# A convolution and feed-forward kernel: the order of the first loads of x, w_in, w_out and the softmax weights

## The chip, the cores and the metric

The kernel runs on one NeuronCore of one Trainium2 chip. The metric is the device time of one execution in microseconds (us). Before the change it is 759.16 us, the median of three runs (757.6 to 759.79).

## What is computed

The first stage is a causal convolution whose weights are given for every position and head: seven logits per head go through a softmax, and the seven last rows of `x` are summed with those weights. The second stage is a feed-forward layer with a squared ReLU.

```python
# x: (8, 4096, 192), weight_gen: (8, 4096, 8 heads, 7 taps), float32
w = softmax(weight_gen, axis=-1)
x_pad = concat([zeros(B, 6, D), x], axis=1)          # causal: rows s-6 .. s
out = einsum('bshk,bskhg->bshg', w, x_unf)           # 24 columns per head
# w_in: (192, 2048), w_out: (2048, 192)
h = maximum(out.reshape(32768, 192) @ w_in, 0)
result = (h * h) @ w_out                             # (32768, 192), float32
```

## The kernel before

**Blocks.** The 32768 tokens are cut into 64 sub-blocks of 512. The first two sub-blocks are blocks of their own (block 0 and block 1), and all later blocks hold two (block 2 has sub-blocks 2 and 3). Matmuls run in f16 with sums in float32.

**Softmax.** The logits are worked off in parts (`Softmax`, L146). The first sequence has four parts of 8 rows on each of 128 partitions; s0, s1 and s2 are the first three. A part is loaded (L172, tile `wg`), put through an exponential on ScalarE (L194, `ex`), summed, inverted and scaled on VectorE (L201, L208, L216). The result of a small part lies in `v_first`, that of a large one in `v_big`. Small parts are then copied within SBUF to rows by position (`wr_load_sbuf`, L307, tile `wr`), half of the copies issued by SyncE and half by GpSimd (`move_rows`, L495).

**Conv.** VectorE multiplies `wr` with a band mask (`st_band`, L325), which gives banded matrices `bd`. TensorE multiplies them with `x` in f16 (`st_conv`, L393, into PSUM `yp`), and ScalarE copies the result to `y` (L404). The x tile `xt` comes in one of two ways: sub-blocks 0 and 1 are loaded as float32 by SyncE into `x_st` (`x_load_f32`, L283; L267, L271 and L277) and cast (`x_cast`, L291), the others are loaded and cast at once by a DMA that GpSimd issues (`x_load`, L279).

**Feed-forward.** A unit (`st_unit`, L409) makes 1024 columns of hidden values: matmuls with `w_i` into PSUM `h` (L418; three buffers, which `yp` shares), ReLU on ScalarE (L427, `t`), square on VectorE (L430, `g`). The second matmul (`st_mm2`, L450) sums `g` with `w_o` into PSUM `o`; ScalarE copies and VectorE adds the halves (L464, L465), and the rows are stored. The squares of block j are used by the second matmuls beside the units of block j+1. A string per block sets the order: u is a unit, M half of a second matmul, C the conv of the next block. The first three are `"uuuuuCuuu"`, `"MuMuuuMuuuMCu"` and `"MuuuuMuuuuMuuuuuuuMCu"`.

**What sets the order.** The schedule is written out by hand. Every engine takes its instructions in the order in which the program emits them, and a DMA is issued by an engine's queue when all ahead of it in that queue has been issued and its own waits are met. The lines ahead of the main loop (L516 to L547) emit the start: SyncE loads s0's logits, w_in's first half, x of sub-block 0, w_in's second half. ScalarE casts both halves of w_in (L532), then SyncE copies each half across the partitions (`cross_w_in`, L125), ScalarE casts x of sub-block 0 (L537), and SyncE loads x of sub-block 1 and s1's logits. The buffer of `x_st` is one (tag `ex`), so the second x load waits for the first cast. GpSimd issues row copies, the four parts of w_out (`load_w_out`, L138, a DMA that casts to f16), and clears `v_big`.

**Within the main loop**, a table of due times (`at`, L558) places the pieces of the later softmax parts: s1's exponential ahead of unit 4 of block 0 and its sum and scale ahead of unit 5; s2's logits are loaded ahead of unit 6 of block 0 by SyncE (L592, L619), its exponentials ahead of units 3 and 5 of block 1, its sums and scales ahead of unit 7 of block 1 and unit 0 of block 2. The bands for sub-blocks 2 and 3 come ahead of units 1 and 3 of block 1.

Of the kernel before, what the change touches and what calls it, by code (L numbers as in the profile page):

```python
# [9 lines left out]
def kernel(  # L10
# [25 lines left out]
    nc = tc.nc  # L36
# [52 lines left out]
    w_i = const.tile([P, WQ, 2, NQ + NQ // 2], f16, name="w_i")  # L89
# [22 lines left out]
    x_st = {}  # L112
# [10 lines left out]
    def cross_w_in(q):  # L123
        for r0, r1 in ((0, RT), (RT, 0)):
            nc.sync.dma_start(out=w_i[r0 : r0 + RT, q, 1], in_=w_i[r1 : r1 + RT, q, 0])  # L125
# [11 lines left out]
    def load_w_out(q, n):  # L137
        nc.gpsimd.dma_start(  # L138
            out=w_o[:, q * NF // n : (q + 1) * NF // n],
            in_=moe_w_out[q * Dff // n : (q + 1) * Dff // n].rearrange(  # L140
                "(c p) m -> p c m", p=P
            ),
        )
# [101 lines left out]
    x_t, wr_t, bd_t, yp_t, y_t, g_t, h_t, t1_t, o_t, o_sb_t = ({} for _ in range(10))  # L245
# [17 lines left out]
    def block_load(j, dst, src, width, eng):  # L263
        t0 = (j % NBB) * TB
        first, last = int(t0 == 0), NT
        if first:
            eng.dma_start(out=dst[:, 0], in_=src[0:P, :])  # L267
        a = t0 + tile_start(j, NT - 1)
        if a != t0 + starts[-1]:
            last = NT - 1  # L270
            eng.dma_start(out=dst[:, last], in_=src[a : a + P, :])  # L271
        ap = rows(src, t0 + starts[first], width)
        ap = bass.AP(
            tensor=ap.tensor, offset=ap.offset,
            ap=[ap.ap[0], [STEP * width, last - first], ap.ap[2]],
        )
        eng.dma_start(out=dst[:, first:last], in_=ap)  # L277
# [5 lines left out]
    def x_load_f32(j):  # L283
        x_st[j] = p_one.tile([P, (R + HALO) * HK], f32, name="x_st", tag="ex")
        block_load(
            j, x_st[j][:, 0 : NT * D].rearrange("p (t d) -> p t d", t=NT), x[j // NBB], D, nc.sync
        )

    def x_cast(j, copy):
        x_t[j] = p_x.tile([P, NT, D], f16, name="xt")  # L290
        copy(out=x_t[j].rearrange("p t d -> p (t d)"), in_=x_st[j][:, 0 : NT * D])  # L291
# [6 lines left out]
    def wr_load_sbuf(j, parts, order, engines):  # L298

        wr_t[j] = p_wr.tile([P, NT, HP, SL * 2], f16, name="wr")  # L300
        n = 0
        for i in order:
            t0 = max(j % NBB * TB + tile_start(j, i), 0)
            for s in parts:
                a, b = max(t0, s.t0), min(t0 + P, s.t0 + P * s.r)
                if a < b:
                    engines[n % len(engines)].dma_start(  # L307
                        out=wr_t[j][a - t0 : b - t0, i].rearrange("p g c -> p (g c)"),
                        in_=s.v[
                            (a - s.t0) // s.r : (b - s.t0) // s.r, HALO : HALO + s.r  # L310
                        ].rearrange("p r g c e -> p r (g c e)"),
                    )
                    n += 1
# [170 lines left out]
    with nc.allow_low_precision("fp16 matmul pipeline"), tc.manual_schedule():  # L484
# [25 lines left out]
        def spin(n):  # L510
# [5 lines left out]
        s0, s1, s2 = parts[:3]  # L516
# [3 lines left out]
        w_st = [  # L520
            p_wg.tile([P, (R + HALO) * HK], f32, name="w_st", tag="wg")[:, 0 : NQ + NQ // 2]
            for q in (0, 1)
        ]
# [4 lines left out]
        s0.total(0, s0.rh)  # L528
        s0.recip(0, s0.rh)
        s0.scale(0, s0.rh, nc.vector)  # L530
        for q in (0, 1):
            nc.scalar.copy(out=w_i[:, q, 0], in_=w_st[q])  # L532
        wr_load_sbuf(0, [s0], (0, 2, 1, 4, 3), (nc.sync, nc.gpsimd))
        wr_load_sbuf(1, [s0], range(NT), (nc.gpsimd,))
        for q in (0, 1):
            cross_w_in(q)
        x_cast(0, nc.scalar.copy)  # L537
        x_load_f32(1)
        s1.load(nc.sync)
        for i in (0, 2, 1, 3, 4):  # L540
            st_band(0, (i,))
        st_conv(0)
        st_bands(1)
        x_cast(1, nc.vector.tensor_copy)
        for q in range(4):
            load_w_out(q, 4)
        nc.gpsimd.memset(v_big, 0.0)  # L547


# [8 lines left out]
        def at(j, u, kind, *args):  # L558
            fill.setdefault((j, u), []).append((kind, *args))
# [14 lines left out]
        def exp_time(j, u):  # L574

            if u == 0:
                return j - 1, 5 if j == 2 else 12
            return j, {1: 0, 7: 3, 9: 4, 15: 8}[u]
# [3 lines left out]
        for n, s in enumerate(parts[2:], 2):  # L582
            b, f = s.b, s.fb
            k = n - min(m for m, p in enumerate(parts) if p.b == b)
            times = TIMES.get((b, k)) or (
                (f - 6, 15), (f - 5, 15), (f - 4, 15), (f - 3, 9), (f - 3, 15)
            )
            pieces = [(lo, min(lo + PIECE, s.rh)) for lo in range(0, s.rh, PIECE)]
            for (j, u), (lo, hi) in zip(times, pieces, strict=True):
                at(*exp_time(j, u), "exp", s, lo, hi)  # L590
                at(j, u, "soft", s, lo, hi)
            at(*((0, 6) if n == 2 else (times[0][0] - 1, 0)), "load", s)  # L592
        for j in range(1, NBLK - 1):
            a = BLOCKS[j + 1][0]
            small = [p for p in parts if p.fb <= j + 1][-1].r == FIRST
# [121 lines left out]
```

The softmax here doesn't subtract the row's maximum and nothing guards it: scores larger than these inputs give would overflow.

## Time and profile before

The profile is one execution under the hardware profiler: a span of 759.6 us, all times in us from its start.

| engine | busy, us | share of the span |
|---|---|---|
| PE (TensorE matmul) | 742.6 | 98% |
| DVE (VectorE) | 625.3 | 82% |
| ACT (ScalarE) | 623.5 | 82% |
| POOL (GpSimd) | 87.2 | 11% |

A matmul's end is modelled, so a PE that is busy isn't always at its peak: at half clock it shows as busy as at full clock. Beside the busy time stands the clock that was granted to TensorE, as a share of the full one. SP is SyncE, and a q after an engine's name stands for its queue, which issues DMAs. An arrow `a <- b` in a line of waits reads "a waited for b". The transfers at the start, by the table of DMA issues (median from issue to landing):

| transfer | issued by | count, KB each | us to landing |
|---|---|---|---|
| `w_st` from w_in | SyncE | 2 x 512, 4 x 128 | 5.1, 6.2 |
| `x_st` from x | SyncE | 2 x 384, 2 x 96 | 6.8, 6.0 |
| `w_i` across partitions | SyncE | 4 x 192 | 4.6 |
| `wg` from weight_gen (small parts) | SyncE | 6 x 392 | 4.2 |
| `w_o` from w_out | GpSimd | 4 x 192 | 7.5 |

### The profile page before, as it was taken

What the parts mean: (1) busy time and instruction counts of PE and PEld (TensorE: products, weight loads), DVE (VectorE), ACT (ScalarE), POOL (GpSimd) and SP (SyncE); (2) the same over time, 40 slices, a digit from 0 to 9 for tenths busy, and PEclk for the clock granted to TensorE, in tenths of its full rate; (3) what the DMA queues carried; (4) which work ended last, traced back from release to release, by engine and by line L of the source; (5) the groups of instructions that cost most, each with busy time, mean ns of one, the idle gap of its engine ahead of it and who ended that gap; (6) DMA issues with size and microseconds to landing.
All of it is one profiled execution on the core that took longest, in us unless ns stands there. A gap on an engine that the chain in (4) does not pass through costs nothing.

```text
span 759.6 us, 33610 instructions
## 1 busy us (share of the span) xinstructions
PE 742.6 (98%) x15266; PEld 576.8 (76%) x15266; DVE 625.3 (82%) x1007; ACT 623.5 (82%) x753; POOL 87.2 (11%) x125
## 2 busy tenths in 40 slices
PE   8789999999999999999999999999999999999998
PEld 4666877877787778877877787787778777777787
DVE  5679999899799988888888888898878987777853
ACT  4578898888889888888888888888888888888873
POOL 6222111011100110010100110001100011000000
PEclk9889999999999999999999999999999999999999
DMA  8554525645325544524445433465432454432312
GB/s 213 101 92 79 120 53 103 135 92 113 77 64 113 107 79 59 91 93 83 79 79 121 92 61 51 78 136 99 67 62 40 78 107 79 59 69 53 50 44 65
DMA packets 122394, 65.22 MB, mean 86 GB/s; under 512 B 83881, under 2 KB 118668, under 8 KB 121740
## 3 DMA queue, kind: packets, MB, share of 16 engines
q1 hardware_dynamic: 78012, 46.46, 22.0%
q0 software_dynamic: 44096, 16.53, 20.2%
q8 instruction: 119, 1.95, 1.1%
q14 instruction: 23, 0.19, 0.1%
q10 hardware_dynamic: 144, 0.10, 0.0%
HBM read 48.61 MB, written 28.70 MB: 102 GB/s over the span
## 4 chain that ended last, share of the span: by engine, by line
PE 88%; DVE 4%; DMA 3%; ACT 2%; SPq 1%; issue 1%; DVEq 0%; ACTq 0%
PE o L450 42%; PE h L418 40%; PE yp L393 6%; DMA wg<-in_weight_gen_dram 2%; DVE g L430 2%; ACT t L427 1%; DVE bd L325 1%; DMA w_st<-in_moe_w_in_dram 1%; DMA vd<-v_big 1%; SPq L307 0%; DVE o_sb L465 0%; DVE rcp L208 0%; DVE ssum L201 0%; SPq L118 0%; DVE v_big L216 0%
## 5 line engine op out<-in xcount | busy, mean ns | idle before, releaser
L427 ACT ACTIVATE t<-h 128x1024 f16<-128x1024 f32 x512 | 497.4, 1027 | 68.7 <-PE h L418 68.6
L430 DVE TENSOR_TENSOR g<-t 128x1024 f16<-128x1024 f16 x512 | 335.1, 688 | 102.6 <-ACT t L427 99.7
L450 PEld LDWEIGHTS <-g 64*128 64x128 f16 x8192 | 357.0, 94 | 51.9 <-issue 4.0
L450 PE MATMUL o<-w_o,g 64*128 64x192 f16 x8192 | 387.4, 243 | 1.8 <-issue 1.0
L418 PE MATMUL h<-y,w_i 64*128 64x512 f16 (+1 forms) x3168 | 381.9, 372 | 5.4 <-ACT t L427 3.8
L418 PEld LDWEIGHTS <-w_i 64*128 64x128 f16 x3168 | 176.5, 95 | 108.6 <-issue 7.1
L325 DVE TENSOR_TENSOR bd<-wr,mask 128x4160 f16<-128x4160 f16 (+3 forms) x89 | 149.5, 1703 | 4.8 <-DMA wr<-v_first 4.8
L277 POOL DMA_DIRECT2D xt<-in_x_dram x62 | 51.3, 832 | 450.4 <-PE yp L393 427.5
L464 ACT COPY o_sb<-o 128x384 f32<-128x384 f32 x129 | 62.3, 483 | 32.9 <-PE o L450 32.9
L465 DVE TENSOR_TENSOR o_sb<-o,o_sb 128x384 f32<-128x384 f32 x129 | 71.2, 552 | 10.1 <-ACT o_sb L464 7.8
L404 ACT CAST y<-yp 128x1024 f16<-128x1024 f32 (+1 forms) x64 | 48.2, 805 | 15.3 <-PE yp L393 15.3
L393 PE MATMUL yp<-bd,xt 128*32 128x104 f16 (+8 forms) x3864 | 52.3, 211 | 5.0 <-DVE xt L291 4.1
L393 PEld LDWEIGHTS <-xt 128*32 128x32 f16 (+3 forms) x3864 | 47.0, 93 | 10.8 <-issue 5.0
L194 ACT ACTIVATE ex<-wg 128x448 f32<-128x448 f32 (+2 forms) x44 | 27.3, 619 | 10.3 <-DMA wg<-in_weight_gen_dram 10.3
L216 DVE TENSOR_TENSOR v_big<-ex,rcp 128x112 f16<-128x112 f32 (+1 forms) x136 | 27.4, 264 | 2.1 <-DMA vd<-v_big 0.9
L201 DVE TENSOR_REDUCE ssum<-ex 128x64 f32<-128x448 f32 (+2 forms) x44 | 26.1, 594 | 2.5 <-ACT ex L194 2.5
L208 DVE RECIPROCAL rcp<-ssum 128x64 f32<-128x64 f32 (+2 forms) x44 | 23.7, 539 | 1.5
L307 POOL DMA_DIRECT2D wr<-v_first x31 | 16.8, 563 | 27.1 <-DVE v_first L216 27.1
L267 POOL DMA_DIRECT2D xt<-in_x_dram x7 | 3.8, 548 | 137.5 <-PE yp L393 137.5
L512 PE MATMUL wp<-warm 128*128 128x512 f16 x42 | 11.6, 446 | 1.3 <-DVE warm L504 1.3
L512 PEld LDWEIGHTS <-warm 128*128 128x128 f16 x42 | 4.6, 112 | 7.7 <-issue 3.0
L216 DVE TENSOR_TENSOR v_first<-ex,rcp 128x112 f16<-128x112 f32 (+1 forms) x48 | 9.1, 256 | 0.3
(16 smaller groups left out, 23.9 us busy)
## 6 DMA issues: line engine op xcount, KB each, us to landing
out_dram<-o_sb SPq DMA_DIRECT2D x63, 384.0 KB, 3.0
xt<-in_x_dram POOLq DMA_DIRECT2D x42, 240.0 KB, 6.3
wg<-in_weight_gen_dram SPq DMA_DIRECT2D x4, 1064.0 KB, 8.2
xt<-in_x_dram POOLq DMA_DIRECT2D x20, 192.0 KB, 5.4
wr<-vd SPq DMA_DIRECT2D x38, 80.0 KB, 4.0
vd<-v_big SPq DMA_DIRECT2D x5, 512.0 KB, 5.7
wg<-in_weight_gen_dram SPq DMA_DIRECT2D x6, 392.0 KB, 4.2
wg<-in_weight_gen_dram SPq DMA_DIRECT2D x3, 616.0 KB, 4.0
```

Of the source, the lines that this page charges most:

```text
L194: nc.scalar.activation(out=self.ex[:, lo:hi].rearrange("p r g k e -> p (r g) k e"), in_=self.wg[:, lo:hi].rearrange("p r (g e) k -> p (r g ...
L216: eng.tensor_tensor(out=bass.AP(tensor=v.tensor, offset=v.offset + lo * H * SL + lo % SL * 2 + g * SL * 2, ap=[list(v.ap[0]), [H * SL + 2, ...
L277: eng.dma_start(out=dst[:, first:last], in_=ap)
L325: nc.vector.tensor_tensor(out=bd_t[j][:, H * lo : H * (lo + len(tiles) * n)].rearrange("p (g m c) -> p g m c", g=shape[1], c=2 * SL), in0= ...
L393: nc.tensor.matmul(out=yps[k // per][p0 : p0 + m, col + a : col + b], lhsT=x_t[s][:, i, 32 * q : 32 * q + m], rhs=bd[:, h // 2, h % 2, a - ...
L404: nc.scalar.copy(out=y[:, k0:k1, 0:th], in_=yp[:, 0 : (k1 - k0) * th].rearrange("p (k c) -> p k c", c=th),)
L418: nc.tensor.matmul(out=h[:, half, jj * th : (jj + 1) * th], lhsT=w_in_chunk(u * per + jj, slot, half), rhs=y_t[j][r0 : r0 + RT, k, 0:th], ...
L427: nc.scalar.activation(out=t1, in_=h, func=ActF.Relu)
L430: nc.vector.tensor_tensor(out=g, in0=t1, in1=t1, op=AluOp.mult)
L450: nc.tensor.matmul(out=oo[:, cc * Dm : (cc + 1) * Dm], lhsT=g[r0 : r0 + RT, cc * P : (cc + 1) * P], rhs=w_o[r0 : r0 + RT, fc, :], start=(f ...
L464: nc.scalar.copy(out=o_sb, in_=o[0][:, c])
L465: nc.vector.tensor_tensor(out=o_sb, in0=o[1][:, c], in1=o_sb, op=AluOp.add)
```

## The change

The first loads are put in another order. ScalarE casts only w_in's first half ahead of x; the cast of x of sub-block 0 comes next, SyncE loads x of sub-block 1 behind the first half's crossing, and only then are w_in's second half cast and crossed. w_out is loaded in two pairs of parts. A memset of one column of the x tile of sub-block 0 ahead of the first pair makes GpSimd wait until the conv of block 0 has read that tile; a memset of one column of the second `x_st` ahead of the second pair makes it wait until that x has landed and been cast. Nothing reads the cleared columns afterwards. s2's logits are loaded by GpSimd behind w_out and no longer by SyncE in the main loop; the parts after it are loaded as before. The aim is to have x of sub-block 1 and the logits of s1 and s2 there before they are due, with w_out out of their way.

```diff
@@ -528,22 +528,28 @@
         s0.total(0, s0.rh)
         s0.recip(0, s0.rh)
         s0.scale(0, s0.rh, nc.vector)
-        for q in (0, 1):
-            nc.scalar.copy(out=w_i[:, q, 0], in_=w_st[q])
+        nc.scalar.copy(out=w_i[:, 0, 0], in_=w_st[0])
         wr_load_sbuf(0, [s0], (0, 2, 1, 4, 3), (nc.sync, nc.gpsimd))
         wr_load_sbuf(1, [s0], range(NT), (nc.gpsimd,))
-        for q in (0, 1):
-            cross_w_in(q)
+        cross_w_in(0)
         x_cast(0, nc.scalar.copy)
         x_load_f32(1)
+        nc.scalar.copy(out=w_i[:, 1, 0], in_=w_st[1])
+        cross_w_in(1)
         s1.load(nc.sync)
         for i in (0, 2, 1, 3, 4):
             st_band(0, (i,))
         st_conv(0)
         st_bands(1)
         x_cast(1, nc.vector.tensor_copy)
-        for q in range(4):
+
+        nc.gpsimd.memset(x_t[0][:, 0, 0:1], 0.0)
+        for q in (0, 1):
             load_w_out(q, 4)
+        nc.gpsimd.memset(x_st[1][:, 0:1], 0.0)
+        for q in (2, 3):
+            load_w_out(q, 4)
+        s2.load(nc.gpsimd)
         nc.gpsimd.memset(v_big, 0.0)
@@ -589,7 +595,8 @@
-            at(*((0, 6) if n == 2 else (times[0][0] - 1, 0)), "load", s)
+            if n > 2:
+                at(times[0][0] - 1, 0, "load", s)
```

## The prediction

> **What bounds the kernel now.** I read the page first (engine rows, slices), then the busy time by stretches, then the waits of the first 70 us, the chain of the first 80 us, and the timeline of SyncE and GpSimd. The page's first part and the table by stretches (columns: length; busy PE, PEld, DVE, ACT, POOL; PE clock; DMA share; GB/s):
>
> ```profile
> PE 742.6 (98%) x15266; PEld 576.8 (76%) x15266; DVE 625.3 (82%) x1007; ACT 623.5 (82%) x753; POOL 87.2 (11%) x125
> ```
>
> ```profile
> 15.00:20.00 5.00, 3.89 (x60) 3.10 (x59) 1.85 (x2) 4.08 (x5) 2.96 (x2) 1.00 1.33 235
> 20.00:25.00 5.00, 1.15 (x64) 1.15 (x68) 1.86 (x4) 0.85 (x2) 0.00 (x0) 0.81 0.75 169
> 25.00:30.00 5.00, 5.00 (x74) 3.80 (x66) 4.86 (x14) 4.56 (x6) 0.00 (x0) 0.51 0.02 3
> 35.00:40.00 5.00, 2.53 (x54) 2.20 (x49) 4.70 (x4) 0.85 (x2) 0.47 (x1) 1.00 1.25 244
> 40.00:45.00 5.00, 3.70 (x44) 3.41 (x43) 3.76 (x6) 4.39 (x6) 0.00 (x0) 0.51 0.08 20
> 100.00:740.00 640.00, 638.79 (x13312) 496.71 (x13310) 539.45 (x849) 543.92 (x658) 55.43 (x74) 1.00 0.42 82
> ```
>
> From 100 us on TensorE idles 1.2 us in 640: no edit of the loads can bring anything there. What is to be had lies before 70 us: two holes in TensorE's work (20 to 24, 37.5 to 41), each followed by some 6 us at half clock. The waits of the first 70 us (total, times, longest) name both:
>
> ```profile
> ACT ex L194 <- DMA wg<-in_weight_gen_dram: 10.3, 3, 4.2
> DVE xt L291 <- DMA x_st<-in_x_dram: 6.3, 1, 6.3
> PE yp L393 <- DVE xt L291: 4.1, 1, 4.1
> PE h L418 <- ACT t L427: 3.8, 1, 3.8
> ```
>
> The chain (start, length, what) and SyncE's timeline say when those transfers were issued:
>
> ```profile
> 12.81 0.46 SPq L125
> 13.31 0.60 SPq L125
> 14.01 0.53 SPq L271
> 14.58 0.49 SPq L277
> 15.12 9.15 DMA wg<-in_weight_gen_dram
> 24.38 0.95 ACT ex L194
> ```
>
> ```profile
> 34.52 0.59 SPq L172 DMA_DIRECT2D wg<-in_weight_gen_dram  x1
> ```
>
> Hole 1: the second x is issued at 14.01 and 14.58, behind the crossing of w_in's second half, which waits for its cast (12.78). It lands 8.5 us later (23.1); the cast on VectorE (L291) and the conv of block 1 wait. s1's weights, issued at 15.12, land at 24.3, and ScalarE, in order, stands at their exponential. Hole 2: s2's weights are issued at 34.52, behind SyncE's copies of s1's rows, which wait until s1 is scaled (30.22); they land at 39.7, and ScalarE stands 4.15 us at that exponential while TensorE waits for its PSUM.
>
> **What the skill says.** "TensorE: Matmul & The Clock Gate", What's actually happening: half clock after an idle window of about 3.4 us, full clock after as much busy time. The trace agrees in kind: idle of 4.07 and 3.77 us is followed by 0.50 from 23 to 29.5 and from 40.4 to 46.9; the idle 0.9 us at 12.8 is not. "DMA: Bandwidth & Descriptors", Issuing engines are not separate DMA queues: all issuers share the same 16 DMA engines. The trace agrees: from 15 to 20 us the GpSimd queue took 89.8% and SyncE's 41.5%, together the 1.33 above. The same page's SWDGE vs HWDGE vs iDMA: only GpSimd can cast in a DMA, and its rings and SyncE's are served in turn. w_out, cast to f16, is what fills GpSimd's queue there.
>
> **The change, part by part.**
>
> *x cast ahead of w_in's second cast.* x_st(0)'s large part is issued at 3.60 and lands after 5.1: 8.7. ScalarE finishes the first w_in cast at 7.27+1.47 = 8.74, casts x until 9.73, and stands ready before w_in's second half lands (11.24). So the reordering costs ScalarE nothing. The conv of block 0 ends as before, at about 14.6: its last band ends at 14.15.
>
> *x of the second sub-block earlier.* It shares x_st's buffer, free at 9.73 instead of 13.68. SyncE is at its three row copies until 10.31, then the first crossing until 11.55; x is issued at 11.6 and 12.15, 2.4 us earlier. Landing: 5.1 us as for the first x (beside full traffic) to 6.5, since two crossings (768 KB) are in flight too, but no w_out: 17.3, bounds 17 and 20. The second crossing then starts at 12.8 as before (its cast ends 12.78), and units 4 to 7 alone need it.
>
> *s1's weights.* Issued at 13.95 instead of 15.12. Landing: with no other large transfer 4.2 us (the median), before 9.15; two of four w_out parts join at 14.9. I take 6 us: 20.0; bounds 18 and 22.
>
> *w_out in two parts.* Two memsets of one column, 0.10 us each (the row of the 128x1 constants). The first waits for the conv of block 0 (14.65): parts 0 and 1 are issued 14.8 to 16.5 (0.80 each). The second waits for VectorE's cast of x(1): bands of block 1 end at 16.84, x lands 17.3, cast 0.66, so 18.0; parts 2 and 3 issued until 19.8. Queued behind it on GpSimd: s2's load, the memset of v_big (2.53), then s1's row copies (not due before 26.1) and x of block 2. Landing 4.5 to 9.5 us as before: part 1 by 23.5, part 3 by 27. The users are the first second-matmuls of block 0 (23.7 and, for parts 2 and 3, 25.7). These take g as well, and g of unit 7 is due at 28.2 by the sum below, so the late half hides behind VectorE.
>
> *s2's weights through GpSimd.* Issued at about 20 instead of 34.5, landing by 27 (3.2 to 9.2 us). Its exponential stands in ScalarE's order at about 31.2. Hole 2 goes. SyncE loses one issue of 0.6 us that nothing waits for.
>
> *The new schedule.* Durations are those of the rows: relu 1.02, square 0.69, unit of block 0 0.65 on TensorE.
> - ScalarE ends relu 3 at 20.22 as before; s1's exponential 20.2 to 21.2 (before 24.38), relu 4, y, relus 5 to 7: the last ends at 26.0 (before 30.34).
> - VectorE: x cast, four squares by 20.9, square 4 at 22.9, s1's sum, reciprocal, scale (0.96+0.85+1.46) until 26.15. Before: 30.22. Gain so far 4.07.
> - Squares 5 to 7 until 28.2, so the second-matmul of block 0 ends at 28.5. Its copy and add, one square, then VectorE waits for s1's rows: before, the band started 5.1 us after the scale (35.30), so 31.2.
> - From there VectorE has no hole: band 2.33, two squares 1.29, band 2.35, four squares 2.76, add 0.56, s2's first piece 2.06, one square 0.69, second piece 1.73: sum 13.8, end at 45.0. Before: 51.98. ScalarE and TensorE run ahead of it: conv of block 2 waits for the second band (37.2; before 45.25).
> - Gain 51.98-45.0 = 7.0 us. The check: between the two scales VectorE was busy 16.37 of 21.76 us; now it takes 18.85, with 2.5 us idle left.
> - After that nothing changes: from 51.98 to 67.5 VectorE was busy 14.87 of 15.52 and ScalarE all of it, and later TensorE is full. The 7.0 us are carried to the end.
>
> TensorE's holes were 4.07+3.77, and half clock cost its matmuls about 3.0 (conv 1.47 against 0.92 and 2.34 against 1.58, second-matmuls 1.89 and 2.79 against 1.48): 10.9 us in all. I expect 7.0 because VectorE becomes the bound from 31 to 45.
>
> 759.16 - 7.0 = 752.2 us.
>
> **Rivals.**
> 1. *The first hole is only shortened.* s1's weights land at 22 or later, as w_out's first parts share the engines, or a rest hole (35.1 to 37.3 before conv 2, 2.2 us in my schedule) grows past 3 us and brings half clock back. For: 1.33 DMA share. Against: half of w_out is held. ScalarE 1.8 us later and 1 us of slow matmuls: gain 3 to 5.5, 755.
> 2. *VectorE isn't the bound.* If rows and bands come earlier, the 2.5 us idle also goes: gain 9 to 9.5, 750.
> 3. *w_out becomes the wait: slower.* If x(1) lands no earlier than before (23.1), the memset holds parts 2 and 3 until 23.9; issued by 25.5, plus 9.5: 35. The second-matmul that ran at 31.45 waits 3.5 us, TensorE falls to half clock again, and the exponential that no longer waits gives back 0.5: 762. For: GpSimd's queue is strictly in order here, and landings reached 9.5. Against: x is issued 2.4 us earlier into engines at 0.4 to 0.9 share (10 to 15 us).
>
> **How the numbers follow.** Forecast 0.58, rival 1 0.24, rival 2 0.06, rival 3 0.12. Faster by over 0.3% means under 756.9: the first three cases less 0.02 of rival 1, and 0.02 of rival 3's milder forms: 0.88. Same: the mild end of rivals 1 and 3, 0.05. Slower 0.07. The range takes rival 2's 749 at one end and reaches through rival 1 to 756.7 at the other; rival 3 is left out.
>
> **What would show it.** In the profile after: x_st's second load issued near 12.1 and landed by 18; conv of block 1 with no hole of 4 us; s1's exponential at 20 to 21; no wait of ScalarE on s2's weights; PE clock 1.00 from 20 to 47; s2's second scale ending near 45; busy shares from 100 us on unchanged. Wrong if a wait on w_o appears at L450, if s1's exponential still starts after 23, or if VectorE, once ahead, idles for rows and loses more than 2.5 us.

## The result and the profile after

The changed kernel takes 753.38 us (median of six; 753.05 to 755.29), the kernel before beside it 758.71 us. The ratio is 0.9938, with a 95% interval of 0.9922 to 0.9955: 4.7 us less by the ratio, 5.3 by the medians. A second measurement, made later beside the last experiments, gave 0.9930 (0.9913 to 0.9948); one of its six executions, the profiled one, took 1976.68 us, is left out of that ratio, and gives no marks below.

The page's first part and the busy time by stretches (length; busy PE, PEld, DVE, ACT, POOL; PE clock; DMA share; GB/s) of the kernel after:

```profile
PE 737.4 (98%) x15266; PEld 562.8 (75%) x15266; DVE 624.4 (83%) x1007; ACT 623.3 (83%) x753; POOL 88.0 (12%) x128
```

```profile
15.00:20.00 5.00, 3.18 (x51) 2.79 (x50) 4.00 (x6) 4.03 (x5) 1.31 (x3) 1.00 1.17 257
20.00:25.00 5.00, 3.83 (x121) 3.23 (x123) 2.42 (x4) 3.40 (x5) 3.28 (x3) 1.00 1.12 203
25.00:30.00 5.00, 4.04 (x85) 3.33 (x82) 4.76 (x14) 3.08 (x5) 2.28 (x5) 1.00 0.09 16
40.00:45.00 5.00, 4.35 (x65) 3.17 (x63) 4.86 (x15) 3.34 (x6) 1.89 (x3) 1.00 0.83 133
100.00:740.00 640.00, 639.91 (x13372) 488.84 (x13368) 538.08 (x850) 544.42 (x658) 55.43 (x74) 1.00 0.42 82
```

The clock is 1.00 in every stretch of this execution, where before it was 0.81 (20 to 25 us), 0.51 (25 to 30) and 0.51 (40 to 45). From 100 us on nothing to speak of has changed. The waits of the first 70 us:

```profile
ACT ex L194 <- DMA wg<-in_weight_gen_dram: 3.6, 2, 1.9
DVE xt L291 <- DMA x_st<-in_x_dram: 1.0, 1, 1.0
PE h L418 <- DMA w_i<-w_i: 1.5, 1, 1.5
```

The wait for x fell from 6.3 to 1.0 us. Of ScalarE's waits for weights that for s2 is gone; 1.7 us for s1 is left. A new wait of 1.5 us is on the second half of w_in's crossing. The chain in order of time (start, length, what) still runs through s1's load, now shorter:

```profile
13.67 0.59 SPq L125
14.31 7.19 DMA wg<-in_weight_gen_dram
21.60 0.12 ACT ex L194
```

And GpSimd's timeline shows when w_out was let go:

```profile
12.92 0.10 POOL L546 MEMSET xt<- 128x1 f16 x1 [0.48 <-PE yp L393]
13.43 1.55 POOL L138 DMA_DIRECT2D w_o<-in_moe_w_out_dram  x2 [0.40 <-issue]
18.55 0.10 POOL L549 MEMSET x_st<- 128x1 f32 x1 [3.57 <-DVE xt L291]
```

The first memset ran at 12.92, while the conv of block 0 was still going on, so w_out's first pair was issued ahead of s1's logits (14.31). The forecast had it at 14.65, behind the conv.

### The profile page after: what moved, and what is told of

Read it like the earlier page. It is cut to its first block, busy times and chain, and to the rows that moved or that the text cites. A ratio compares the mean times of both kernels' runs of the same rounds, so it can differ in the third digit from the quotient of the medians.

```text
span 751.2 us, 33616 instructions
## 1 busy us (share of the span) xinstructions
PE 737.4 (98%) x15266; PEld 562.8 (75%) x15266; DVE 624.4 (83%) x1007; ACT 623.3 (83%) x753; POOL 88.0 (12%) x128
## 4 chain that ended last, share of the span: by engine, by line
PE 91%; DVE 4%; DMA 2%; SPq 1%; issue 1%; ACT 0%; POOL 0%; DVEq 0%; ACTq 0%
PE o L450 44%; PE h L418 42%; PE yp L393 6%; DVE g L430 1%; DMA wg<-in_weight_gen_dram 1%; DMA wr<-v_first 1%; DVE v_first L216 1%; DVE bd L325 1%; SPq L307 0%; DVE ssum L201 0%; DVE rcp L208 0%; SPq L125 0%; POOL wr L307 0%; DVE o_sb L465 0%; ACT ex L194 0%
## 5 line engine op out<-in xcount | busy, mean ns | idle before, releaser
L450 PEld LDWEIGHTS <-g 64*128 64x128 f16 x8192 | 351.7, 94 | 56.5 <-issue 3.7
L418 PE MATMUL h<-y,w_i 64*128 64x512 f16 (+1 forms) x3168 | 377.7, 370 | 4.2 <-DMA w_i<-w_i 1.5
L418 PEld LDWEIGHTS <-w_i 64*128 64x128 f16 x3168 | 167.0, 94 | 112.9 <-issue 4.8
L216 DVE TENSOR_TENSOR v_big<-ex,rcp 128x112 f16<-128x112 f32 (+1 forms) x136 | 27.4, 264 | 2.5 <-DMA vd<-v_big 1.3
```

Of the source, the lines that this page charges most:

```text
L216: eng.tensor_tensor(out=bass.AP(tensor=v.tensor, offset=v.offset + lo * H * SL + lo % SL * 2 + g * SL * 2, ap=[list(v.ap[0]), [H * SL + 2, ...
L418: nc.tensor.matmul(out=h[:, half, jj * th : (jj + 1) * th], lhsT=w_in_chunk(u * per + jj, slot, half), rhs=y_t[j][r0 : r0 + RT, k, 0:th], ...
L450: nc.tensor.matmul(out=oo[:, cc * Dm : (cc + 1) * Dm], lhsT=g[r0 : r0 + RT, cc * P : (cc + 1) * P], rhs=w_o[r0 : r0 + RT, fc, :], start=(f ...
```

## The experiments

The names in the table are explained one by one below it. All marks are read from the timelines, each of one profiled execution. That of order_only (758.84 us) is the slowest of its kernel's 22, those of hold_conv (751.83) and soft_first (750.11) are the fastest of theirs, and that of s1_early (754.96) is 1.7 us under its median. "The mark" is the start of the first unbroken second matmul of block 3; from there TensorE is full in every kernel, and the rest of the span is 690.1 to 692.1 us in all profiles, with no order in it that follows the edits. Gains are (1 - ratio) x 759 us, with the interval worked out the same way. s2_only to order_s2 ran on one chip; hold_conv, s1_early, no_recip and before_again on a second; hold_conv_2, soft_first, warm_hole2 and the second measurement of after on a third. Each gain is against executions of before on the same chip. The half clock is twice the missing share of the granted clock times the span, as a mean over the timed executions.

| kernel | s1's exponential | s1's scale ends | s2's scale ends | mark | gain, us | half clock, us |
|---|---|---|---|---|---|---|
| before | 24.38 | 30.23 | 51.98 | 67.52 | | 9.4 to 10.3 |
| before_again | 24.60 | 30.62 | 49.16 | 64.30 | | |
| after | 21.60 | 27.43 | 45.10 | 61.10 | 4.7 (3.4 to 5.9), again 5.3 (3.9 to 6.6) | 1.8, 3.3 |
| s2_only | 25.30 | 31.14 | 49.13 | 64.26 | 2.0 (1.4 to 2.7) | 6.1 |
| order_hold | 21.21 | 27.05 | 47.03 | 62.58 | 3.0 (2.1 to 3.9) | 4.8 |
| order_only | 23.27 | 29.11 | 50.64 | 66.16 | 2.0 (1.3 to 2.7) | 7.4 |
| order_s2 | 23.16 | 28.99 | 46.68 | 61.81 | 3.8 (2.6 to 4.9) | 4.3 |
| hold_conv | 20.13 | 25.98 | 43.48 | 58.62 | 6.2 (4.9 to 7.4) | 1.8 |
| hold_conv_2 | 21.29 | 27.12 | 44.76 | 59.90 | 6.2 (4.6 to 7.9) | 2.5 |
| s1_early | 22.64 | 28.47 | 46.23 | 61.37 | 3.0 (1.8 to 4.3) | 7.5 |
| no_recip | 21.05 | 25.99 | 43.00 | 59.22 | 6.4 (5.0 to 7.7) | 2.5 |
| soft_first | 20.03 | 24.36 | 41.25 | 56.61 | 8.4 (7.1 to 9.8) | 1.8 |
| warm_hole2 | 24.39 | 30.23 | 49.16 | 64.30 | 1.3 (0.7 to 2.0) | 6.0 |

**The parts of the change.** The theory was that the two holes lie one after the other in one chain. The first kernel has only the load of s2 moved.

```diff
 (the kernel before)
             load_w_out(q, 4)
+        s2.load(nc.gpsimd)
         nc.gpsimd.memset(v_big, 0.0)
...
-            at(*((0, 6) if n == 2 else (times[0][0] - 1, 0)), "load", s)
+            if n > 2:
+                at(times[0][0] - 1, 0, "load", s)
```

> The kernel before with one edit: s2's logits are loaded by GpSimd behind the four unheld parts of w_out. Theory (the two holes lie one after the other in one chain, and their gains add): s1's scale still ends near 30.2 us, ScalarE no longer waits for s2, s2's scale ends near 48 instead of 52, gain 4.0 us, TensorE's clock drops once. Rival (one waiting time absorbs the other): gain under 1.5 us.

ScalarE's timeline of this kernel:

```profile
25.30 0.93 ACT L194 ACTIVATE ex<-wg 128x784 f32<-128x784 f32 x1 [4.97 <-DMA wg<-in_weight_gen_dram]
36.02 0.62 ACT L194 ACTIVATE ex<-wg 128x448 f32<-128x448 f32 x1
```

The wait ahead of s2's exponential is gone, as forecast, and the stretch from s1's scale to s2's is 17.99 us against 21.75 in the first profile of before. But the gain is 2.0 us and not 4.0: the theory was right on the wait and wrong on what the wait cost. The second profile of before and the last experiment below say why. s1's own exponential came 0.9 us later than in the first profile of before and 0.7 later than in the second; that one more load shares the engines is a possible cause and wasn't tried apart.

The next kernel has the rest of the change: order and hold, with s2 loaded as before.

```diff
 (the kernel after)
-        s2.load(nc.gpsimd)
...
-            if n > 2:
-                at(times[0][0] - 1, 0, "load", s)
+            at(*((0, 6) if n == 2 else (times[0][0] - 1, 0)), "load", s)
```

> The kernel after with s2's logits loaded by SyncE as before. Theory: s1's scale ends near 27.4 as after, ScalarE waits for s2's logits some 4 us, gain 2.5 to 3 us in all. Rival (the new order carries the whole change): gain 5 us.

s1's scale ended at 27.05, ScalarE stood 3.75 us at s2's exponential, the gain is 3.0 us: as the theory said. Together with 2.0 for s2's load that is 5.0, and the whole change brought 4.7 and 5.3 in its two measurements. Within these intervals the parts add.

Two kernels without the memsets ask what the hold is worth: one without s2's early load, one with it.

```diff
 (order_hold, and the kernel after)
-        nc.gpsimd.memset(x_t[0][:, 0, 0:1], 0.0)
...
-        nc.gpsimd.memset(x_st[1][:, 0:1], 0.0)
```

> New order of the casts and of x, w_out's four parts not held, s2's logits by SyncE. Theory (x comes earlier because it is issued earlier, s1's logits stay late because w_out shares the DMA engines): x lands near 18.5, s1's exponential at 23 to 24, gain 0.5 to 1.5 us. Rival (the order alone carries the first hole, the hold is worth nothing): s1's exponential at 21.5, gain 2.5 to 3 us.

> The kernel after without the two memsets: w_out's four parts are issued at once, then s2's logits. Theory: s1's exponential at 23 to 24 instead of 21.6, gain 1.5 to 2 us smaller than the whole change. Rival (the hold is worth nothing): the same gain as the whole change within 0.5 us.

In both s1's exponential starts at 23.2, as the theory said, 1.6 us later than in the kernel after, and x was cast near 20 instead of 17.8. The gains are 2.0 and 3.8 us: about 1 us less than their counterparts with the hold (3.0, and 4.7 or 5.3). The order alone was sized too low (0.5 to 1.5). The intervals overlap in both pairs, so the worth of the hold in time isn't shown clear of noise. What is shown is that s1's exponential shifts the same way in both, by 2.1 and 1.6 us.

**What the first memset waits for.**

```diff
 (the kernel after)
-        nc.gpsimd.memset(x_t[0][:, 0, 0:1], 0.0)
+        nc.gpsimd.memset(x_t[0][:, NT - 1, D - 1 : D], 0.0)
```

> The kernel after, but the first memset clears the last column of the last tile of x of sub-block 0, so GpSimd waits for the end of the conv of block 0 and not for its first matmuls. Theory (w_out's first pair, issued at 13.4 and so ahead of s1's logits at 14.3, is what made them land at 21.5): w_out is issued from 14.5, s1's logits land by 20.5, the crossing of w_in's second half by 19, s1's scale ends near 26.3, gain 1 us over the kernel after. Rival (the pair isn't what delays them): landings within 0.3 us of the kernel after and the same time.

GpSimd's and ScalarE's timelines of this kernel:

```profile
14.44 0.10 POOL L546 MEMSET xt<- 128x1 f16 x1 [2.06 <-PE yp L393]
14.95 1.56 POOL L138 DMA_DIRECT2D w_o<-in_moe_w_out_dram  x2 [0.40 <-issue]
```

```profile
20.13 0.95 ACT L194 ACTIVATE ex<-wg 128x784 f32<-128x784 f32 x1 [0.16 <-DMA wg<-in_weight_gen_dram]
```

A column of the tile's last part makes the memset wait 1.5 us longer. s1's logits, issued at 14.27, landed 5.8 us later; in the kernel after it was 7.2. TensorE's wait for w_in's crossing fell from 1.5 to 0.4 us, and s1's scale ended at 25.98, near the prediction's 26.15. So it was the early release that made s1's logits late. Three other profiles agree: in order_hold and no_recip, where the pair's first part is issued ahead of the logits as well, they took 6.6 us, and in soft_first, where it is issued behind them, 5.6. The time was measured again beside the kernel after:

> The kernel after, unchanged, beside the three below on one chip. Theory: gain 4.5 to 5.5 us as at first, s2's scale 17.7 us after s1's.

> The kernel after with its first memset on the last column of the last tile of x, again, for a comparison with the kernel after on the same chip. Theory (w_out's first pair ahead of s1's logits cost 1.3 us): 1 to 2 us faster than the kernel after. Rival (the two earlier measurements differ by the chip): within 0.5 us of it.

On one chip the ratios are 0.9930 (0.9913 to 0.9948) for the kernel after and 0.9918 (0.9896 to 0.9940) for this one, 0.9 us apart. The first measurements of the two, which weren't made side by side, were 1.5 us apart. Both lean the same way, but the intervals overlap: that the logits land earlier is shown, the size of the gain isn't. In this execution the logits landed after 6.1 us, at 20.3, but s1's exponential started only at 21.29, and with no wait for them. The table by stretches says what came in between:

```profile
15.00:20.00 5.00, 4.31 (x50) 3.88 (x51) 3.79 (x5) 3.22 (x4) 3.05 (x5) 0.66 1.15 260
```

The clock was at half from 16 to 19.5, units took longer, and the four relus ahead of the exponential ended 1.4 us later than in the first execution of hold_conv. Of the 1.4 us, 0.4 is from bands that began later; the rest of what was won on the transfer was lost on the clock.

**s1's logits much earlier.**

```diff
 (the kernel after)
         load_w_in(w_st[1], 1, nc.sync)
+        s1.load(nc.sync)
...
-        s1.load(nc.sync)
```

> The kernel after with s1's logits loaded right behind w_in's second half (SyncE's queue is empty from 5.7 to 8.3 us). Theory (s1's landing is the only thing that holds ScalarE at 20 us): the exponential starts at 20.2, s1's scale ends near 26.2, gain 1.2 us over the kernel after. Rival (the 392 KB push w_in's second half and the row copies of block 0 back, as the engines are full from 5 to 10 us): units and bands of block 0 start 1 us later and the gain is gone.

The theory fell and the rival held, by a route that it didn't name in full. The bands of block 0 started at 12.41 instead of 11.33, as the row copies landed later, and TensorE's warm-up had ended by then. The kernel's table by stretches and ScalarE's timeline:

```profile
15.00:20.00 5.00, 4.11 (x70) 3.37 (x60) 3.63 (x5) 2.41 (x3) 2.54 (x5) 0.50 1.14 220
```

```profile
22.64 0.94 ACT L194 ACTIVATE ex<-wg 128x784 f32<-128x784 f32 x1
```

The exponential waited for no transfer, yet it started 1.0 us later than in the kernel after, since the units began 1.3 us later and, at half clock, fed the relus slowly. The gain of 3.0 us is below the 4.7 and 5.3 of the change itself, which weren't measured beside it; the intervals overlap in part.

**Is VectorE the pace-maker?**

```diff
 (the kernel after)
         def recip(self, lo, hi):
+            if self in parts[1:3]:
+                self.rcp = self.ssum
+                return
             nc.vector.reciprocal(out=self.rcp[:, lo:hi], in_=self.ssum[:, lo:hi])
```

> The kernel after without the three reciprocals of s1 and s2 (their weights are scaled by the sum and not by its inverse, a part of the computation left out). They take 0.86 + 0.56 + 0.47 = 1.9 us of VectorE. Theory (VectorE sets the pace from s1's sum until 61 us): s2's scale ends 1.9 us earlier, near 43.2, and the kernel is 1.9 us faster than the kernel after. Rival (ScalarE, TensorE or the landing of the row copies set the pace after s1's scale): at most the 0.9 us of s1's reciprocal arrive.

The gain is 6.4 us, 1.1 to 1.7 more than that of the kernel after, but that wasn't measured beside it, and the intervals overlap. In the profile s2's scale ended at 43.00, and the mark came at 59.22, 1.88 us earlier. But s1's exponential was 0.55 us earlier in this execution, so 1.33 of the 1.88 is the edit's. From s1's scale to s2's, 0.66 of the 1.03 us taken away arrived; most of the rest went into VectorE's wait for s1's rows, 1.7 us instead of 1.3. From s1's scale to the mark it is 0.44 against the kernel after, but hold_conv, hold_conv_2 and s1_early, which keep the reciprocals, need less for that way (32.6 to 32.9 us) than this kernel (33.2). So VectorE sets the pace up to s2's scale, beside its wait for the rows. That any of this gain is left at the mark isn't shown: behind s2's scale ScalarE is busy all of 16.22 us in this profile. The theory holds in part.

**The kernel before, profiled again.**

> The kernel before, unchanged, for a second profile: the first was of an execution 2.3 us above the median. Theory (the start varies by the landings of the transfers): block 3's first second-matmul starts 1 us or more earlier than the 67.5 us of the first profile. Rival (the later part varies): 67.5 again, and less time after it.

The mark is at 64.30 and no longer at 67.52, and what follows it takes the same time (691.9 and 692.1). The start varies. Its two stretches around the second hole, to be set beside the 0.51 of the first profile:

```profile
35.00:40.00 5.00, 2.57 (x56) 2.27 (x51) 4.17 (x4) 1.55 (x3) 0.85 (x2) 1.00 1.15 238
40.00:45.00 5.00, 4.35 (x178) 4.00 (x179) 4.75 (x8) 5.00 (x8) 0.35 (x1) 1.00 0.20 26
```

ScalarE waited 3.5 us for s2 here, too, and TensorE stood 3.1 us. But the clock stayed at 1.00, and s2's scale ended 18.5 us after s1's, only 0.9 us more than in the kernel after, where there is no hole.

**The second hole without its half clock.**

```diff
 (the kernel before, main loop)
                     run_fill(j, u)
+                    if (j, u) == (1, 6):
+                        for i in range(28):
+                            nc.tensor.matmul(
+                                out=o[0][:, 384:512], lhsT=warm[:, 0:P], rhs=warm[:, 0:P],
+                                start=True, stop=True, skip_group_check=True,
+                            )
                     st_unit(j, u)
```

The idle matmuls write to the PSUM bank in which a second matmul's sum is open, and the output changes with them.

> The kernel before with 28 idle matmuls of 128 columns, into unused columns of PSUM, ahead of unit 6 of block 1: they fill TensorE's second hole (3.1 to 3.8 us) and change no wait. s2's logits still come late. Theory (ScalarE's wait for s2 lies beside VectorE's bands, and what costs is the half clock that often follows): clock stays at 1.00 from 40 to 46, s2's scale ends 18.5 us after s1's instead of 20 to 21.8, gain about 2 us, as much as loading s2 early alone brought. Rival (the wait itself costs): gain under 0.7 us.

TensorE's timeline around the hole and the table by stretches of this kernel:

```profile
37.12 1.74 PE L662 MATMUL o<-warm 128*128 128x128 f16 x28
40.64 0.83 PE L418 MATMUL h<-y,w_i 64*128 64x256 f16 x12 [1.78 <-ACT t L427]
```

```profile
40.00:45.00 5.00, 4.36 (x178) 3.98 (x179) 4.09 (x8) 5.00 (x8) 0.39 (x1) 1.00 0.17 25
```

The filling took 1.74 us and left a hole of 1.78. No wait was taken away; ScalarE still stood 3.83 us at s2's exponential. The clock held, s2's scale ended 18.9 us after s1's, and the gain is 1.3 us (0.7 to 2.0), between theory and rival. s2's scale and the mark came at 49.16 and 64.30, as in the second profile of before, where the clock held by itself. The early load of s2 alone brought 2.0 us (1.4 to 2.7). The intervals overlap, so the share can't be told closely, but a good part of what that load brings can be had by holding the clock and leaving the wait as it is. The profile says the same: without half clock the wait makes the stretch between the scales 0.9 us longer than in s2_only (17.99), since most of it lies beside VectorE's bands.

**A version that is faster than both.** In the profile of hold_conv VectorE stands 0.96 us for relu 4 ahead of s1's sum, which needs only s1's exponential. The last kernel has the later release of w_out, and the sum, reciprocal and scale of s1 one unit earlier:

```diff
 (hold_conv)
-        at(0, 5, "soft", s1, 0, s1.rh)
+        at(0, 4, "soft", s1, 0, s1.rh)
```

> As the one before, and s1's sum, reciprocal and scale stand ahead of unit 4 and no longer ahead of unit 5, so VectorE does them before unit 4's square. Theory (VectorE sets the pace and idled 1 to 2 us for that square): s1's scale ends 1.5 us earlier, near 24.4, and the kernel is 1 to 1.5 us faster than the one before. Rival (ScalarE or TensorE sets the pace by then): no gain over 0.3 us.

VectorE's timeline:

```profile
18.39 2.49 DVE L430 TENSOR_TENSOR g<-t 128x1024 f16<-128x1024 f16 x4
21.01 0.97 DVE L201 TENSOR_REDUCE ssum<-ex 128x112 f32<-128x784 f32 x1
22.01 0.85 DVE L208 RECIPROCAL rcp<-ssum 128x112 f32<-128x112 f32 x1
22.90 1.46 DVE L216 TENSOR_TENSOR v_first<-ex,rcp 128x112 f16<-128x112 f32 x8
```

The sum starts at 21.01 instead of 22.63, s1's scale ends at 24.36 (forecast 24.4), and everything behind it moves along: 750.85 us, ratio 0.9889 (0.9871 to 0.9907). That is 8.4 us under the kernel before by the ratio. It is 2.2 more than hold_conv_2 on the same chip, where the intervals still overlap, and 3.1 more than the kernel after on that chip, where they don't.

## Why the prediction was right or wrong

752.2 us was forecast and 753.38 measured, inside the range. The gain was put at 7.0 us and is 4.7 to 5.3. The direction, the place (before 70 us) and the two waits were right. By its steps:

- *x cast ahead of w_in's second cast, at no cost.* Right: the casts ran 7.26, 8.64 and 11.04, and ScalarE was waiting for w_in's second half in between.
- *x of sub-block 1.* Right: issued at 12.23 (12.15), landed at 17.7 (17.3).
- *w_out's first pair held behind the conv of block 0.* Wrong. The prediction put the memset at 14.65, the end of the conv; it cleared a column of the tile's first part, which the conv's first matmuls read, and ran at 12.92. The pair was then in flight ahead of s1's logits. That landing was sized at 6 us and took 7.2; with the release where the prediction had it, it took 5.8 and 6.1. s1's scale ended at 27.4 and not at 26.15. The wait of 1.5 us for w_in's crossing, which the prediction didn't have, comes mostly from the same cause, since it fell to 0.4 us with the later release. It lies beside ScalarE's wait for s1.
- *w_out's second pair hidden.* Right: the second matmul waited 0.8 us for g and never for w_o.
- *s2's load through GpSimd.* Right: no wait ahead of its exponential.
- *s2's scale at 45.0.* It ended at 45.1, but by luck, as two errors cancel: s1's scale 1.3 us late, the stretch to s2's scale 17.7 us instead of 18.85.
- *"Before: 51.98", and the 3.0 us of half clock after holes.* This is the term of the sum that was mis-sized. The prediction took one profile's half clock as what a hole always costs. That profile was of an execution of 761.48 us, 2.3 above the median of its measurement. In the second one the same hole was 0.7 us shorter and left the clock alone, and s2's scale ended at 49.16. Against the first profile the mark moved by 6.4 us, against the second by 3.2, and the measured 4.7 to 5.3 lies between. Taking 7.0 from a median of 759.16 mixed the two.
- *Nothing changes after s2's scale.* Nearly: the way to the mark took 16.0 us instead of 15.5. From the mark to the end it took 690.1 us, in the two profiles of before 692.1 and 691.9. What makes this 2 us isn't known; the other kernels lie in between.

Of the rivals, the first (the first hole only shortened, as s1's logits come late) was partly true. s1's exponential started at 21.60, outside the 20 to 21 that was to show the forecast. The cause is the one that this rival names, w_out's first parts, and its gain, 3 to 5.5 us, is the measured one. Its half clock didn't come in this execution. The other two didn't come up: no wait for w_o appeared, and no_recip shows that VectorE carries weight between the two scales. A slip in a reading changes nothing: the two queue shares, 89.8% and 41.5%, make 1.31, and the rest of the 1.33 is instruction fetch (1.3%).

What stays open is how much of the gain is clock. Over the executions of before that were timed beside the experiments, those with a mean clock under 0.992 took 760.4 us and those above 0.9945 took 758.4, and from before to after the half clock falls from some 10 to 2 or 3 us. But only the second hole was tried by itself.

## What to carry to other kernels

A memset put in as a gate waits only for those who touch the bytes that it clears: to gate on the end of a stage, clear bytes that its last instruction reads. A profile of one execution shows one draw of what varies from run to run, here TensorE's clock around a hole; before such a stretch is priced, compare the profiled execution with the median, or profile a second. And when a wait is removed, look for work that stands behind another wait in program order only: moving s1's sum ahead of a square that it doesn't need, together with the later release, brought more than 3 us beyond the change.

## What the runs showed of the hardware that was not expected

Half clock doesn't need a hole of 3 us. In hold_conv_2 and s1_early the longest time that TensorE stood between 11 and 16.6 us was 0.9 and 1.1 us. TensorE was busy 2.40 of 3.5 us from 12.0 to 15.5 in the one and 1.30 of 3.0 from 12.0 to 15.0 in the other, with short matmuls, and the clock fell to 0.50 for some 3.5 and 7 us. In hold_conv, with 2.22 of 3.5 us busy, it stayed at 1.00. The stretches of hold_conv_2 and hold_conv (length, busy PE, PE clock, DMA share, GB/s), and the longest time that TensorE stood in order_hold before its first half clock (20.6 to 24.3 us):

```profile
12.00:15.50 3.50, 2.40 (x76) 1.00 0.83 192
12.00:15.50 3.50, 2.22 (x79) 1.00 0.88 203
```

```profile
20.49 0.95 PE L418 MATMUL h<-y,w_i 64*128 64x256 f16 x9 [1.21 <-DMA w_i<-w_i]
```

So a thin stretch can do what a hole does, in some executions and not in others. "TensorE: Matmul & The Clock Gate", What's actually happening, in the Trainium skill says that the windows run freely and don't start with the kernel, which would fit the change from one execution to the next; no run here shows the windows themselves.

The same section puts the drop after an idle window of about 3.4 us, and here the runs agree only in part. Each of the holes of 3.4 to 4.6 us came with half clock, and those of 3.07 us (before_again) and 2.13 us (no_recip) didn't. But holes of 2.30 us in order_only and 2.53 us in order_s2 were followed by half clock too, and in warm_hole2 it began 1.5 us into a hole of 3.99 us. The measurements decide: the length of a hole alone doesn't tell, and no bound can be read from these runs.
